# Four d_ff tiles beside the attention instead of five, the first input in two transfers, the low half of a pair in two pieces, and the sums added by 128 tokens

## The chip, the cores and the metric

The kernel runs on one core of a Trainium2 chip. Its time is the device time of one execution in microseconds (us). TensorE (PE in the profile) multiplies matrices, VectorE (DVE), ScalarE (ACT) and GpSimd (POOL) do elementwise work, and SyncE (SP) issues nearly all transfers.

## The reference

The input is a recurrence over 768 tokens for 4 sequences and 8 heads of 40 channels, and behind it a gated feed-forward layer on all 3072 tokens, with weights in 64-bit floats:

```python
for t in range(S):
    y[:, :, t] = np.einsum('bhd,bhde->bhe', rt, state)
    Sa = np.einsum('bhde,bhe->bhd', state, at)
    state_decay = state * wt[:, :, None, :] - np.einsum('bhd,bhe->bhde', Sa, bt)
    state = state_decay + np.einsum('bhd,bhe->bhde', vt, kt)
...
x = attn_out.transpose(0, 2, 1, 3).reshape(B * S, H * D)   # 3072 x 320
out = ((x @ w_a) * (x @ w_b)) @ w_out                      # d_ff = 1536
```

## The kernel before

**Blocks and batches.** The 768 tokens are cut into 12 blocks of 64. A block has 4 batches (one for each sequence), so the attention has 48 batches; the text counts them in the order in which they end. A batch goes through `prep` (two scans for the decay products, the scaled operands `A` and `BK`, the score matrix `pssc`, masked into `TT`), then the four batches of a block together through `lanes` (a triangular solve of 31 steps on VectorE, `Yt` and `psl`, with a way through device memory to turn the data, and the products `psw` and `pst`), then through `main` (`psr`, `psu`, `psg`, `psy`, and last the transposes `psyt`). `self_state` carries the state to the next block (`pss`, `psst`). When four batches of a block have ended, `xform` splits their output into a high and a low part in `xkr`, which holds two blocks.

**The feed-forward layer.** d_ff is cut into 12 tiles of 128. A unit is one tile for one block (256 tokens): 16 matmuls into `ab` (8 for w_a, 8 for w_b, by parts of the operands), a copy on ScalarE, the product on VectorE, a cast to the high part `gh` on ScalarE, the low part `gl` on GpSimd, and 6 matmuls into `po`. This text calls it a single. A `Pair` takes two blocks at once (512 tokens): 16 matmuls of 512 columns, and 12 into four banks. The first `F1` tiles are held in `ws1` from the start and run as singles while the attention runs, as far as a block's output is there; blocks 0 and 1 take only 2 and 3 of them then (`FIRST`) and the others later. Their sums go to device memory (`po_d`). After the attention the other tiles follow in groups of two (`groups`, in three sets of weights that are filled in turn), nearly all as pairs, and VectorE adds their sums onto the earlier ones (`fin2`, `acc`). Each tile of weights is decoded from 64-bit floats to two 32-bit parts by VectorE, ScalarE and GpSimd (`decode`, `w_ex`, `w_mt`, `w_rs`).

**What sets the order.** The class `Order` plans while the program is built: each part of the work is a generator that yields the engine and the tiles that its next step needs, and `run` takes the step that could start first by the plan's clock, plus a claim that puts it back (`after` with `WAY` and `NWAY` puts preparations of later blocks back; `LATER` the loading of weights). The engines then run their instructions in this order. Where the plan sees TensorE idle for over 0.8 us (`GAP`), `warm` puts matmuls of the identity with itself into the queue, into the tile that comes next (`pssc<-ident`, `ab<-ident`); their result is overwritten. This text calls them fillers. In the trace each filler is two records.

`F1`, `groups`, `all_units` and `moe` set which tile runs when; `prep` loads `I`; `Pair.whole` makes `gl` and ends a group; all of these carry lines of the change.

Of the kernel before, what the change touches and what calls it, by code (L numbers as in the profile page):

```python
# [10 lines left out]
F32 = mybir.dt.float32  # L11
# [9 lines left out]
B = 4  # L21
# [3 lines left out]
HB = 32  # L25
# [4 lines left out]
P = 128  # L30
NF = DFF // P
CW = NG * (C + 1)
PW = CW + 1 + NG * 3 * C
F1 = 5
FG = 2
# [3 lines left out]
NL = 12  # L39
WAY = 0.5  # L40
LATER = 1.5
NWAY = 1
URG = 0.05
NEAR = 0.05
FIRST = (2, 3)
AHEAD = 3
SPB = 2
# [5 lines left out]
VC = 0.2  # L53
WARM = 12
RAW = 2

# [4 lines left out]
SPARE = 1.0  # L61
HOP = 0.1
LAND = 2.4
# [11 lines left out]
class Order:  # L75
# [78 lines left out]

    def part(self, gen):
        self.parts.append([gen, None])
        self.step(self.parts[-1])
# [7 lines left out]
    def run(self):  # L165
        while self.parts:
            best = None
            for p in self.parts:
                e, deps, claim, may = p[1]
                if may is not None and not may():  # L170
                    continue
                at = max([self.now[e]] + [self.ready(x, e) for x in deps])
                t = at + (claim(at) if callable(claim) else claim)
# [130 lines left out]
def wkv_moe(ctx, tc, pin, rv, vn, wa, wb, wo, out):  # L304
    nc0 = tc.nc
    order = Order(tc, nc0)
    nc = order.nc
# [212 lines left out]
    class Pair(Unit):  # L520
# [16 lines left out]
        def whole(self):  # L537
# [142 lines left out]
    def prep(q):  # L680
# [79 lines left out]
    def lanes(n):  # L760
# [20 lines left out]
        done.blocks += 1  # L781
        yield "scalar", [nb0_d[n], nb1_d[n]], 0.0, lambda: done.at > SPB
        ps = at_take("psl")
        nc.scalar.copy(out=ps, in_=yid)
        Y = ps.rearrange("p (i t) -> p i t", t=HB)
        for s in range(HB - 1):
            ni, w = s // 2 + 1, HB - 1 - s
            Wv = W[:, 0:ni * w].rearrange("p (i t) -> p i t", i=ni)
            yield "vector", [N, Y], urgent, None
            nc.vector.tensor_mul(  # L790
                out=Wv, in0=Y[:, 0:ni, s:s + 1].to_broadcast([P, ni, w]),
                in1=N[:, s:s + 1, s + 1:].to_broadcast([P, ni, w]))
            yield "vector", [], urgent, None
            nc.vector.tensor_sub(out=Y[:, 0:ni, s + 1:], in0=Y[:, 0:ni, s + 1:], in1=Wv)
        yield "scalar", [Y], 0.0, None

        Y = N[:, 0:HB // 2]
        nc.scalar.copy(out=Y.rearrange("p i t -> p (i t)"), in_=ps)
        at_give(ps)
        eng = nc.scalar if n < TSQ else nc.sync  # L800
# [60 lines left out]
    def main(q):  # L861
# [49 lines left out]
        order.part(self_state(q, uvf, bkf, stf, st, sdf))  # L911
        yield "scalar", [ps, ps0], 0.0, None
# [51 lines left out]
    def self_state(q, uvf, bkf, stf, st, sdf):  # L964
        n, b = divmod(q, B)
        if n < NS - 1:
            yield "tensor", [uvf, bkf], 0.0, lambda: done.at > 0
            ps = at_take("pss")
# [62 lines left out]
    def fin2(n, last):  # L1031
        def f(po):
            for hf in range(2):
# [31 lines left out]
    def moe():  # L1065
# [3 lines left out]
        for n, kk, f, first, last, fin in all_units():  # L1069
            if isinstance(n, tuple):  # L1070
# [5 lines left out]
                u = Pair(lp[0], f"{n[0]}_{f}", x, dest(f), first, last, fin, 0.06)  # L1076
                order.part(u.whole())
                while not u.begun:
# [18 lines left out]
            u.by = "scalar" if kk < 0 else "vector"  # L1097
            order.part(u.whole())
            while not u.begun:
# [74 lines left out]
    for q in range(NS * B):  # L1174
        order.part(prep(q))
    for n in range(NS):
        order.part(lanes(n))
    for q in range(NS * B):
        order.part(values(q))
        order.part(others(q))  # L1180
        order.part(main(q))
    for n in range(NS):
        order.part(xform(n))
    order.part(all_weights())
    order.part(moe())
    order.part(early())
    order.part(late())
    order.part(judge())
# [101 lines left out]
```

## Time and profile before

| | |
|---|---|
| three runs | 956.69, 960.84 and 963.85 us, median 960.84 us |
| profiled execution | 963.8 us |
| its span, first to last instruction | 961.6 us, so 2.2 us lie around it |
| mean granted TensorE clock | 0.964 |
| PE, DVE, ACT, POOL busy | 927.0, 586.5, 436.8, 299.5 us |
| end of the last batch's transposes | 695.1 us into the span |

The busy time of PE counts the fillers. A matmul's record is longer than the time until the next one starts, since they overlap; so the time that a group of matmuls takes in the queue is read from the chain of waits, where a row gives the start and the length of a run of them. Nearly every row names line 190, the helper that records each operation, so rows are told apart by their tiles.

### The profile page before, as it was taken

What the parts mean: (1) busy time and instruction counts of PE and PEld (TensorE: products, weight loads), DVE (VectorE), ACT (ScalarE), POOL (GpSimd) and SP (SyncE); (2) the same over time, 40 slices, a digit from 0 to 9 for tenths busy, and PEclk for the clock granted to TensorE, in tenths of its full rate; (3) what the DMA queues carried; (4) which work ended last, traced back from release to release, by engine and by line L of the source; (5) the groups of instructions that cost most, each with busy time, mean ns of one, the idle gap of its engine ahead of it and who ended that gap; (6) DMA issues with size and microseconds to landing.
All of it is one profiled execution on the core that took longest, in us unless ns stands there. A gap on an engine that the chain in (4) does not pass through costs nothing.

```text
span 961.6 us, 23562 instructions
## 1 busy us (share of the span) xinstructions
PE 927.0 (96%) x9230; PEld 833.0 (87%) x9230; DVE 586.5 (61%) x1588; ACT 436.8 (45%) x1325; POOL 299.5 (31%) x405
## 2 busy tenths in 40 slices
PE   9999998999897999999999999999999999999996
PEld 9998977898786888888888889888999898888885
DVE  6877687668857767685869494723523646542333
ACT  4164456445663554655565655435533333322221
POOL 2130222123352332242323222213444445442221
PEclk9999989599995999999999999999999999999999
DMA  5454627464734553554655654347477411100013
GB/s 135 123 118 93 146 59 155 104 118 126 161 96 111 122 145 81 113 116 117 145 117 130 143 124 85 97 89 189 119 173 191 104 43 54 49 4 1 1 47 122
DMA packets 132946, 102.56 MB, mean 107 GB/s; under 512 B 86659, under 2 KB 118595, under 8 KB 132827
## 3 DMA queue, kind: packets, MB, share of 16 engines
q1 hardware_dynamic: 130747, 100.71, 44.6%
q8 instruction: 75, 1.23, 0.6%
q10 hardware_dynamic: 2080, 0.26, 0.2%
q14 instruction: 44, 0.36, 0.1%
HBM read 77.03 MB, written 21.94 MB: 103 GB/s over the span
## 4 chain that ended last, share of the span: by engine, by line
PE 73%; DVE 11%; DMA 5%; SPq 3%; issue 3%; POOL 3%; ACT 2%; DVEq 0%; POOLq 0%
PE ab L190 26%; PE po L190 9%; PE pssc L190 8%; PE psr L190 5%; PE psy L190 5%; PE psg L190 4%; PE ps L190 4%; SPq L190 3%; DVE psl L190 3%; DVE Yt L190 3%; PE pss L190 3%; PE psu L190 2%; DMA I<-in_pin_dram 2%; PE psw L190 2%; PE pst L190 2%
## 5 line engine op out<-in xcount | busy, mean ns | idle before, releaser
L190 POOL TENSOR_TENSOR gl<-asb,gh 128x256 fp32r<-128x256 f32 (+1 forms) x106 | 103.0, 972 | 253.7 <-ACT gh L190 241.6
L190 PE MATMUL ab<-xkr,wt 120*128 120x256 f32 (+1 forms) x1024 | 149.5, 298 | 0.0
L190 DVE TENSOR_TENSOR asb<-ab,asb 128x256 f32<-128x256 f32 (+1 forms) x104 | 53.3, 513 | 149.5 <-PE ab L190 88.9
L190 PE MATMUL ab<-xk,wt 120*128 120x512 f32 (+1 forms) x656 | 142.1, 368 | 0.0
L190 PEld LDWEIGHTS ab<-xkr,wt 120*128 120x128 f32 x1024 | 133.6, 192 | 4.9
L190 PEld LDWEIGHTS ab<-xk,wt 120*128 120x128 f32 x656 | 112.7, 188 | 19.1
L190 PE MATMUL po<-wo,gh 128*128 128x320 f32 x424 | 116.4, 322 | 4.5 <-ACT gh L190 4.4
L190 DVE TENSOR_TENSOR Yt<-psl,N 128x126 f32<-128x126 f32 (+22 forms) x372 | 94.1, 253 | 24.5 <-DMA N<-nb_d 13.1
L190 DVE TENSOR_TENSOR psl<-psl,Yt 128x126 f32<-128x126 f32 (+22 forms) x372 | 97.1, 261 | 11.6
L190 ACT CAST gh<-asb 128x256 fp32r<-128x256 f32 (+1 forms) x106 | 51.3, 484 | 110.2 <-DVE asb L190 109.0
L190 ACT COPY asb<-ab 128x256 f32<-128x256 f32 (+1 forms) x106 | 47.7, 450 | 106.3 <-PE ab L190 104.9
L190 PEld LDWEIGHTS po<-wo,gh 128*128 128x128 f32 x424 | 76.4, 190 | 7.8 <-ACT gh L190 5.2
L190 PE MATMUL po<-wo,gl 128*128 128x320 f32 x212 | 67.8, 320 | 5.5 <-POOL gl L190 5.3
L190 ACT ACTIVATE Abd<-A,m 120x192 f32<-120x192 f32 x144 | 54.9, 447 | 31.5 <-POOL A L190 29.4
L190 POOL TENSOR_TENSOR pe<-Pc,rp 120x192 f32<-120x192 f32 x44 | 25.2, 573 | 137.2 <-DVE rp L190 130.7
L190 PE MATMUL pssc<-ident 128*128 128x128 f32 x548 | 65.1, 280 | 1.4 <-POOL ident masks.py:199 1.4
L190 PEld LDWEIGHTS pssc<-ident 128*128 128x128 f32 x548 | 63.7, 196 | 1.6 <-POOL ident masks.py:199 1.4
L190 POOL TENSOR_TENSOR ST<-tmp,pcm 120x360 f32<-120x360 f32 x40 | 33.5, 837 | 94.3 <-DVE tmp L190 94.3
L190 PE MATMUL psg<-rvt 120*128 120x192 f32 (+1 forms) x288 | 53.0, 329 | 0.2 <-DVE tmp L190 0.2
L190 PE MATMUL pssc<-Abd,BK 120*128 120x192 f32 (+1 forms) x288 | 52.1, 319 | 1.1 <-ACT Abd L190 0.9
L190 DVE TENSOR_TENSOR TT<-pssc,tri 128x512 f32<-128x512 f32 x48 | 32.8, 686 | 29.3 <-PE pssc L190 29.2
L190 PEld LDWEIGHTS psg<-rvt 120*128 120x128 f32 x288 | 49.3, 205 | 0.9 <-DVE tmp L190 0.4
(131 smaller groups left out, 1774.0 us busy)
## 6 DMA issues: line engine op xcount, KB each, us to landing
rvt<-in_rv_dram SPq DMA_DIRECT2D x48, 450.0 KB
I<-in_pin_dram SPq DMA_DIRECT2D x46, 361.9 KB
xk_d<-xkr SPq DMA_DIRECT2D x11, 720.0 KB
xk<-xk_d SPq DMA_DIRECT2D x10, 720.0 KB
N<-nb_d SPq DMA_DIRECT2D x48, 128.0 KB
wraw<-in_wa_dram SPq DMA_DIRECT2D x12, 360.0 KB
wraw<-in_wb_dram SPq DMA_DIRECT2D x12, 360.0 KB
wraw<-in_wo_dram SPq DMA_DIRECT2D x12, 320.0 KB
```

Of the source, the lines that this page charges most:

```text
L190: r = fn(*args, **kwargs)
```

## The change

- `F1` is 4: four tiles are held and run as singles beside the attention; the other eight make four groups of two (before: seven, in three groups of two and one of one). Of the 144 tile-and-block products, 56 are singles and 88 lie in 44 pairs; before, 68 were singles and 76 lay in 38 pairs.
- The plan's numbers change: `WAY` 0.5 to 0.25, `NWAY` 1 to 2, `HOP` 0.1 to 0.13, `AHEAD` 3 to 4 (how many blocks ahead sums and inputs are loaded again after the attention).
- The first batch's input `I` (772 columns) comes in two transfers, the first 196 columns (which the scans read) and the other 576.
- In a pair, GpSimd makes `gl` in two halves of 256 columns.
- At the end of a pair's group, VectorE's step of adding two banks is planned as two steps of one bank (128 tokens) each, and a block's output transfer is put into SyncE's queue when its second bank is added.
- `HAND`, `CS` and `PLN` are new means to move a part by hand or to solve on GpSimd; with `{}`, `0.0` and `()` they move nothing.

```diff
-F1 = 5
+F1 = 4
...
-WAY = 0.5
+WAY = 0.25
 LATER = 1.5
-NWAY = 1
+NWAY = 2
...
-AHEAD = 3
+AHEAD = 4
...
+HAND = {}
+CS = 0.0
+PLN = ()
...
-HOP = 0.1
+HOP = 0.13
...
-            nc.gpsimd.tensor_sub(out=gl, in0=g, in1=gh.bitcast(F32))
+            for c in range(2):
+                sl = slice(c * 256, c * 256 + 256)
+                nc.gpsimd.tensor_sub(out=gl[:, sl], in0=g[:, sl], in1=gh[:, sl].bitcast(F32))
...
-                po, then = Unit.po, []
-                for i in range(2):
-                    yield "vector", po[2 * i:2 * i + 2], 0.0, None
-                    then.append(self.done[i](po[2 * i:2 * i + 2]))
+                po = Unit.po
+                for i in range(4):
+                    yield "vector", [po[i]], 0.0, None
+                    then = self.done[i // 2](po[i // 2 * 2:][:2], (i % 2,))
+                    if then and i % 2:
+                        nc.sync.dma_start(out=then[0], in_=then[1])
                 at_give(*po[2:])
                 Unit.po_free, Unit.po = True, None
-                for x in then:
-                    if x:
-                        nc.sync.dma_start(out=x[0], in_=x[1])
...
-        nc.sync.dma_start(out=I, in_=pin[n, b])
+        if q == 0:
+            nc.sync.dma_start(out=I[:, 0:CW + 1], in_=pin[n, b][:, 0:CW + 1])
+            nc.sync.dma_start(out=I[:, CW + 1:], in_=pin[n, b][:, CW + 1:])
+        else:
+            nc.sync.dma_start(out=I, in_=pin[n, b])
```

The change reorders TensorE's queue from the first block on. Behind the fourth batch (the end of block 0) TensorE's queue reads as follows before; `pssc` and `psn` with `Abd` and `BK` are the preparation of batches of a later block, `psyt` ends a batch, and the rows with `ident` alone are fillers:

```order
L190 MATMUL psyt<-ident,yn 120x64
L190 MATMUL pssc<-ident 128x128 x24
L190 MATMUL pssc<-Abd,BK 128x192 x2
L190 MATMUL pssc<-Abd,BK 128x128
L190 MATMUL psn<-ident,BK 128x120 x3
L190 MATMUL pssc<-ident 128x128 x23
L190 MATMUL pssc<-Abd,BK 128x192 x2
L190 MATMUL pssc<-Abd,BK 128x128
L190 MATMUL psn<-ident,BK 128x120 x3
L190 MATMUL pssc<-ident 128x128 x15
L190 MATMUL pssc<-Abd,BK 128x192 x2
L190 MATMUL pssc<-Abd,BK 128x128
```

And now, at the same place (`psw` and `pst` with `TT_173` belong to the solve of block 1):

```order
L193 MATMUL psyt<-ident,yn 120x64
L193 MATMUL psw<-ident 128x128 x3
L193 MATMUL psw<-W,TT_173 32x32 x16
L193 MATMUL psn<-ident,BK 128x120 x3
L193 MATMUL psw<-ident 128x128 x11
L193 MATMUL psw<-W,TT_173 32x32 x16
L193 MATMUL pssc<-ident 128x128 x11
L193 MATMUL pssc<-Abd,BK 128x192 x2
L193 MATMUL pssc<-Abd,BK 128x128
L193 MATMUL pst<-TT_173,W 32x32 x32
```

The products that finish block 1's solve stood behind several preparations of a later block and the fillers ahead of them (they do not come within these rows before); now only the second half of one preparation (`psn`) and one other preparation stand among them.

SyncE's queue begins before with whole inputs, `I` twice and then into the tiles `N` and `W`, and then the first weights and the first scores on their way to device memory:

```order
L190 DMA I<-in_pin_dram 120x772 x2
L190 DMA N<-in_pin_dram 120x772
L190 DMA W<-in_pin_dram 120x772
L190 DMA wraw<-in_wa_dram 120x768
L190 DMA wraw<-in_wb_dram 120x768
L190 DMA nb_d_115<-TT_172 32x5x32
```

And now:

```order
L193 DMA I<-in_pin_dram 120x196
L193 DMA I<-in_pin_dram 120x576
L193 DMA I<-in_pin_dram 120x772
L193 DMA N<-in_pin_dram 120x772
L193 DMA W<-in_pin_dram 120x772
L193 DMA wraw<-in_wa_dram 120x768
L193 DMA wraw<-in_wb_dram 120x768
```

One transfer more stands in front of the second batch's input; the rest keeps its place.

More of the change, by code (lines that the diff above doesn't have):

```diff
@@ L153, in tile, with part @@
         return x
-    def part(self, gen):
-        self.parts.append([gen, None])
+    def part(self, gen, key=""):
+        self.parts.append([gen, None, HAND.get(key, 0.0)])
         self.step(self.parts[-1])
@@ L781, in lanes @@
         done.blocks += 1
-        yield "scalar", [nb0_d[n], nb1_d[n]], 0.0, lambda: done.at > SPB
-        ps = at_take("psl")
+        solver = "gpsimd" if n in PLN else "vector"
+        eng = getattr(nc, solver)
+        if n in PLN:
+            yield "scalar", [nb0_d[n], nb1_d[n]], 0.0, None
+            ps = order.tile(pp, [P, HB // 2 * HB], F32, tag="Y", name="Y", bufs=1)
+        else:
+            yield "scalar", [nb0_d[n], nb1_d[n]], 0.0, lambda: done.at > SPB
+            ps = at_take("psl")
         nc.scalar.copy(out=ps, in_=yid)
@@ L788, in lanes @@
             Wv = W[:, 0:ni * w].rearrange("p (i t) -> p i t", i=ni)
[L789 to L790 removed]
+            yield solver, [N, Y], urgent, None
+            eng.tensor_mul(
                 out=Wv, in0=Y[:, 0:ni, s:s + 1].to_broadcast([P, ni, w]),
                 in1=N[:, s:s + 1, s + 1:].to_broadcast([P, ni, w]))
[L793 to L794 removed]
+            yield solver, [], urgent, None
+            eng.tensor_sub(out=Y[:, 0:ni, s + 1:], in0=Y[:, 0:ni, s + 1:], in1=Wv)
         yield "scalar", [Y], 0.0, None
         Y = N[:, 0:HB // 2]
[L798 to L799 removed]
+        if n in PLN:
+            Y = ps.rearrange("p (i t) -> p i t", t=HB)
+        else:
+            nc.scalar.copy(out=Y.rearrange("p i t -> p (i t)"), in_=ps)
+            at_give(ps)
         eng = nc.scalar if n < TSQ else nc.sync
@@ L910, in main @@
             transp(uT[g], uvf[p0:p0 + C, g * PK:(g + 1) * PK], C, p0)
-        order.part(self_state(q, uvf, bkf, stf, st, sdf))
+        order.part(self_state(q, uvf, bkf, stf, st, sdf), f"s{n}")
         yield "scalar", [ps, ps0], 0.0, None
@@ L966, in self_state @@
         if n < NS - 1:
-            yield "tensor", [uvf, bkf], 0.0, lambda: done.at > 0
+            yield "tensor", [uvf, bkf], CS * (n < 1), lambda: done.at > 0
             ps = at_take("pss")
@@ L1031, in fin2, with f @@
     def fin2(n, last):
-        def f(po):
-            for hf in range(2):
+        def f(po, hfs=range(2)):
+            for hf in hfs:
                 nc.vector.tensor_add(out=acc[n][:, hf, :], in0=po[hf][:, 0:DM], in1=acc[n][:, hf, :])
@@ L1076, in moe @@
                 u = Pair(lp[0], f"{n[0]}_{f}", x, dest(f), first, last, fin, 0.06)
-                order.part(u.whole())
+                order.part(u.whole(), f"u{n[0] if isinstance(n, tuple) else n}.{f}")
                 while not u.begun:
@@ L1097, in moe @@
             u.by = "scalar" if kk < 0 else "vector"
-            order.part(u.whole())
+            order.part(u.whole(), f"u{n[0] if isinstance(n, tuple) else n}.{f}")
             while not u.begun:
@@ L1174, in wkv_moe @@
     for q in range(NS * B):
-        order.part(prep(q))
+        order.part(prep(q), f"p{q // B}")
     for n in range(NS):
-        order.part(lanes(n))
+        order.part(lanes(n), f"l{n}")
     for q in range(NS * B):
-        order.part(values(q))
-        order.part(others(q))
-        order.part(main(q))
+        order.part(values(q), f"v{q // B}")
+        order.part(others(q), f"v{q // B}")
+        order.part(main(q), f"m{q}")
     for n in range(NS):
[L1183 to L1187, printed above, removed]
+        order.part(xform(n), f"x{n}")
+    order.part(all_weights(), "w")
+    order.part(moe(), "u")
+    order.part(early(), "e")
+    order.part(late(), "e")
     order.part(judge())
```

2 lines of the change are left out of this document (1 added, 1 removed).

## The prediction

> **What bounds the kernel now.** I read the page first, for who is busy when.
>
> ```profile
> span 961.6 us, 23562 instructions
> PE 927.0 (96%) x9230; PEld 833.0 (87%) x9230; DVE 586.5 (61%) x1588; ACT 436.8 (45%) x1325; POOL 299.5 (31%) x405
> PE   9999998999897999999999999999999999999996
> PEclk9999989599995999999999999999999999999999
> PE 73%; DVE 11%; DMA 5%; SPq 3%; issue 3%; POOL 3%; ACT 2%; DVEq 0%; POOLq 0%
> ```
>
> PE is busy nearly everywhere, and the chain of waits (last row) runs through it for 73%. But PE's queue holds fillers, so a busy PE is not yet a limit. I therefore cut the span at the end of every fourth batch (the last `psyt` of a block; the rows of blocks 4 and 11 are left out) and at the end of the attention, 695.1 us. The columns are the stretch, its length, busy time of PE, PEld, DVE, ACT and POOL with their instructions, the granted clock, the transfers' share and GB/s.
>
> ```profile
> 0.00:92.60 92.60, 89.33 (x954) 85.31 (x954) 68.38 (x200) 40.39 (x132) 18.89 (x52) 1.00 0.50 117
> 92.60:169.00 76.40, 70.25 (x793) 63.73 (x792) 57.23 (x163) 38.13 (x124) 22.88 (x37) 0.95 0.58 121
> 169.00:237.80 68.80, 67.57 (x723) 60.19 (x722) 49.45 (x149) 30.69 (x99) 17.54 (x24) 0.80 0.49 111
> 237.80:285.40 47.60, 43.12 (x524) 37.68 (x525) 35.41 (x83) 29.10 (x95) 21.64 (x30) 0.96 0.59 139
> ...
> 339.80:409.30 69.50, 67.41 (x781) 62.14 (x782) 44.92 (x136) 36.51 (x120) 20.14 (x30) 0.98 0.46 108
> 409.30:460.60 51.30, 49.80 (x640) 44.36 (x640) 36.62 (x111) 29.19 (x100) 16.10 (x24) 1.00 0.51 119
> 460.60:508.10 47.50, 46.72 (x602) 41.03 (x604) 34.27 (x100) 29.82 (x102) 13.46 (x22) 0.96 0.58 131
> 508.10:558.00 49.90, 49.10 (x553) 43.53 (x554) 35.05 (x106) 28.58 (x96) 15.31 (x24) 1.00 0.56 126
> 558.00:615.40 57.40, 56.95 (x733) 51.08 (x735) 40.55 (x128) 30.92 (x101) 14.56 (x21) 1.00 0.42 98
> 615.40:652.40 37.00, 37.00 (x510) 32.54 (x512) 12.02 (x32) 16.73 (x57) 7.26 (x9) 1.00 0.48 108
> ...
> 742.00:955.00 213.00, 212.06 (x1108) 186.14 (x1106) 98.10 (x196) 59.71 (x105) 78.89 (x68) 1.00 0.18 48
> ```
>
> Counted in the program, 453 of the 472 fillers stand ahead of the 24th batch (409.3 us), none from there to the 40th (615.4 us). So there are three stages. Up to 409 us PE waits for others, with fillers in the gaps; VectorE, 57.2 of 76.4 us in block 1, is the busiest of those. From 409 to 695 us PE is full of real work, 46.7 of 47.5 us in block 7 and 57.0 of 57.4 us in block 9, and VectorE is at 70 to 72% in blocks 6 to 9 (35.05/49.9, 34.27/47.5). After the attention PE is full too (212.06 of 213.00 us), the others are far from it.
>
> **Singles against pairs.** The chain of waits gives what a run of matmuls takes in PE's queue. Two rows for singles, four for pairs:
>
> ```profile
> 716.26 1.91 PE ab L190 x16
> 718.17 0.88 PE po L190 x6
> ...
> 897.50 3.65 PE ab L190 x16
> 901.15 0.88 PE po L190 x6
> 902.04 0.88 PE ps L190 x6
> 902.92 3.65 PE ab L190 x16
> ```
>
> A single is 1.91 + 0.88 = 2.79 us; a pair is 902.92 - 897.50 = 5.42 us, 2.71 for each block. Twelve singles become six pairs: 6 x 5.42 - 12 x 2.79 = 32.5 - 33.5 = **-1.0 us**. So the fifth tile is nearly only moved. Counted in the program, 41 singles begin ahead of the 48th batch's end in place of 50, which takes 9 x 2.79 = 25.1 us out of the attention; behind it stand 15 singles and 44 pairs in place of 18 and 38, which puts back 32.5 - 8.4 = 24.1 us. The removed singles are those of the PE-bound stage: 33 began there before, now 24, four in each block in place of 3 to 8.
>
> The Trainium skill ("TensorE: Matmul & The Clock Gate", Back-to-back issue gap) gives sustained spacings of about 81 ns at 128 columns and 131 ns at 512; by it, with an estimated 98 ns at 256, the change would save 12 x 16 x 98 - 6 x 16 x 131 ns = 6.2 us on `ab`. The rows here contradict it: 3.65 us for 16 is 228 ns at 512 columns, so this gets no chance of its own.
>
> **Fillers and order.** The program now has 460 fillers, not 472. Their price is that of the longest run of them, in the chain (188 records of 94 fillers and 6 others):
>
> ```profile
> 34.08 21.87 PE pssc L190 x194
> ```
>
> 21.87/194 = 0.113 us a record, two records a filler: 0.225 us. Twelve fewer are **-2.7 us**. They also move: 35 in place of 110 within block 1, 413 in place of 453 up to the 24th batch (-9.0 us), then 47 in place of 19 (+6.3 us). A filler says only that a gap was foreseen; I take the net, since a gap that is foreseen wrongly shows as a wait instead. What block 1 loses in fillers it loses because the end of its solve stands earlier. Before, the preparations that stood ahead of it waited for inputs, as the chain shows at that place:
>
> ```profile
> 111.98 3.70 DMA I<-in_pin_dram
> 119.45 4.11 DMA I<-in_pin_dram
> 123.57 2.40 DMA nb_d<-TT
> ```
>
> Those preparations come later now, so that their waits move behind block 1 rather than vanish; the fillers that blocks 2 and 3 gain (71 for 54, 27 for 1) say the same.
>
> **The fifth tile's decoding.** VectorE's five steps for twelve tiles (36 pieces):
>
> ```profile
> L190 DVE SCALAR_TENSOR_TENSOR w_rs<-wraw,w_ex 120x384 f32<-120x384 uint32 (+1 forms) x36 | 23.0, 639 | 0.0
> L190 DVE SCALAR_TENSOR_TENSOR w_ex<-wraw,w_ex 120x384 int32<-120x384 int32 (+1 forms) x36 | 22.0, 612 | 5.4 <-ACT w_ex L190 5.1
> L190 DVE TENSOR_TENSOR w_mt<-w_ex,w_mt 120x384 int32<-120x384 int32 (+1 forms) x36 | 20.1, 559 | 0.5
> L190 DVE TENSOR_SCALAR w_ex<-wraw 120x384 int32<-120x384 int32 (+1 forms) x36 | 20.1, 558 | 3.0 <-DMA wraw<-in_wa_dram 2.6
> L190 DVE TENSOR_SCALAR w_mt<-wraw 120x384 int32<-120x384 int32 (+1 forms) x36 | 16.6, 460 | 20.2 <-POOL wt L190 16.7 <-POOL wo L190 3.4
> ```
>
> 101.8/12 = 8.5 us a tile leave VectorE's early stage and go behind the attention, where VectorE is busy 98 of 213 us; there they cost nothing while the tile is ready a group ahead. In the early stage they are worth between 0 (done in gaps) and 8.5 us. I take 0 beyond the fillers, since the plan already counts a lighter VectorE in them. The tile's three loads move with it; they are in SyncE's queue, ahead of other inputs, within the same bounds.
>
> **The start.** VectorE's first scan waits for the whole first input:
>
> ```profile
> 0.82 0.87 SPq L190 DMA_DIRECT2D I<-in_pin_dram  x2
> 4.53 0.60 DVE L190 TENSOR_TENSOR_SCAN Pc<-I,one 120x195 f32<-120x195 f32 x1 [4.53 <-DMA I<-in_pin_dram]
> 7.17 0.56 DVE L190 TENSOR_TENSOR_SCAN Pc<-I,one 120x195 f32<-120x195 f32 x1
> ```
>
> The first transfer now has 196 of 772 columns. If the time to landing (4.53 - 0.82 = 3.71 us) went by size, the scan would start 2.8 us sooner; if size did not matter, not at all. The second batch's scan, at 7.17, needs an input that is issued one transfer (0.87/2 = 0.43 us) later, and that bounds what follows: -1.2 to +0.4 us, and I take **-0.6 us**. The other 576 columns, which the first batch's `A` reads, have the same bytes in front of them as before.
>
> **The end.** Behind the last pair's last products PE waits for `gl`:
>
> ```profile
> 951.83 1.27 POOL L190 TENSOR_TENSOR gl<-asb,gh 128x512 fp32r<-128x512 f32 x1 [4.20 <-ACT gh L190]
> 953.15 0.42 PE L190 MATMUL po<-wo,gl 128*128 128x320 f32 x1 [0.94 <-POOL gl L190]
> L190 POOL TENSOR_TENSOR gl<-asb,gh 128x256 fp32r<-128x256 f32 x68 | 53.2, 782 | 134.6 <-ACT gh L190 122.5 <-ACT rvt L190 9.0 <-DMA UV<-in_vn_dram 2.8
> ```
>
> A half takes 0.78 us in place of 1.27: **-0.5 us**; the second half ends 1.56 us after 951.83, at 953.39, when PE's third group (0.88 us after 952.66) needs it at 953.54. Elsewhere a pair costs GpSimd 1.56 - 1.27 = 0.29 us more, 44 pairs some 13 us, in a stage where it is busy 79 of 213 us and PE has the next unit's `ab` in between: 0. Adding by 128 tokens has the same additions in the same order at the end, and each output still waits for its second one: 0. `AHEAD` brings loads forward in a stage where PE waits 0.9 us in all: 0.
>
> **The sum**: -1.0 - 2.7 - 0.6 - 0.5 = -4.8 us. The profiled execution took 963.8 us, 3.0 us over the median of the three, so it would be 959.0; against the median, 960.84 - 4.8 = **956.0 us**.
>
> **Rivals.**
>
> *The early stage gains more* (faster). Up to 409 us VectorE and the inputs set the time. If all of the 8.5 us of decoding leave the path there, on top of the sum, it is 956.0 - 8.5 = 947.5 us. For it: VectorE at 75% in block 1 with PE on fillers. Against it: 40 fillers fewer there are already in the sum's -2.7.
>
> *The cover is lost* (slower). From 409 to 695 us singles fill PE while the attention's chain waits for ScalarE, VectorE and inputs. The nine singles that leave are 25.1 us. If PE then waits for the chain in part of this time, the attention does not shorten by it, while the 24.1 us behind it are paid in full. For it: block 3, with three singles and two records of fillers, had 43.1 of 47.6 us busy, and DVE at 74%. Against it: blocks 7 and 10, with three singles each, had PE busy for 46.7 of 47.5 and 37.0 of 37.0 us. It turns the sign when 4.8 of the 25.1 us stay as waits; with two thirds, 16.7, the time is 972.7 us.
>
> *The clock falls.* These rows of 40 us have a low clock; the chain's rows show the same kind of matmuls inside and outside of such a stretch:
>
> ```profile
> 160.00:200.00 40.00, 36.77 (x390) 32.17 (x391) 27.60 (x89) 16.26 (x53) 8.16 (x13) 0.66 0.51 107
> 280.00:320.00 40.00, 34.84 (x388) 29.37 (x383) 26.81 (x90) 18.95 (x60) 9.57 (x14) 0.74 0.43 101
> 147.17 1.48 PE psr L190 x22
> 177.66 7.39 PE psr L190 x53
> ```
>
> 67 ns a matmul become 139 ns. With 75 fillers fewer in block 1 another stretch of some 27 us at half clock ((1 - 0.66)/0.5 x 40) can come. PE's work in it would last 13.6 us longer, half of which, 6.8 us, I count, since PE waits for others early: 962.8 us. The Trainium skill ("TensorE: Matmul & The Clock Gate", HAM oscillation) says that an idle gap over about 3.4 us throws the clock back to half; it speaks against taking fillers out. The trace agrees in part: in both low rows PE is idle, for 3.2 and 5.2 of 40 us, though no row shows the length of a single gap.
>
> **How the numbers follow.** Chances: forecast 0.45 (its own range 949 to 963: the start's and the fillers' bounds, and waits that come out a few us otherwise), early gain 0.26 (943 to 952), cover lost 0.15 (966 to 982), clock 0.14 (959 to 970). The three runs lie 0.75% apart, so about 1% (9.6 us: under 951.2 or over 970.4) can be told from no change. Faster by over 1%: nearly all of the early gain and a quarter of the forecast's own range, 0.24 + 0.11 = 0.35. Slower by over 1%: most of the lost cover and a little of the clock, 0.13. Within: 0.52. The range 941 to 970 leaves out the upper part of the lost cover (0.13) and the far end of an early gain (0.05).
>
> **What would show it.** Cutting the new trace at the same batches: the 24th batch should end some 4 to 10 us before 409, the attention near 695.1 - 25.1 - 2.7 = 667 us, and from there PE should be full for 955.0 - 695.1 + 24.1 = 284 us. Lost cover shows as PE's busy share falling under 95% in blocks 6 to 10; the clock as a row under 0.9 that wasn't there; an early gain as a 24th batch before 398 us. If PE waits for `wt` of a late group, the tile's decoding was not free. The prediction is wrong if the attention ends later than 680 us or the stage behind it is not some 24 us longer.

## The result and the profile after

| | kernel before | changed kernel |
|---|---|---|
| median of 20 runs each, taken together | 961.53 us (956.69 to 968.14) | 966.56 us (961.51 to 974.4) |
| ratio, 95% interval | | 1.0067 (1.0046 to 1.0089) |
| profiled execution, its span | 963.8, 961.6 us | 970.14, 968.1 us |
| end of the 24th, 40th, 44th, 48th batch | 409.3, 615.4, 652.4, 695.1 us | 384.3, 573.3, 641.1, 679.0 us |

The change made the kernel slower by 0.7%, where 0.5% faster was forecast. The time is inside the range, but the sign is wrong. The chip has a second, slower state that a few executions fall into; ratios and intervals, here and below, leave these out and medians do not, so that a ratio need not be the quotient of two medians. The page of the changed kernel:

```profile
span 968.1 us, 23364 instructions
PE 928.1 (96%) x9110; PEld 831.2 (86%) x9110; DVE 594.2 (61%) x1582; ACT 435.2 (45%) x1313; POOL 305.6 (32%) x443
PE   9997999998999999999998999799999999999997
PEclk9997899998989999999999799679999999999999
```

It reads almost like the page of before, but for a hole in the 26th of the 40 slices: PE at 7 tenths, and a granted clock of 6 tenths there and 7 in the next. The cut at the ends of every fourth batch (columns as in the prediction; the rows of blocks 2 to 7 are left out) puts it in its place:

```profile
0.00:107.50 107.50, 100.00 (x980) 95.09 (x980) 83.17 (x235) 43.49 (x138) 26.34 (x60) 0.92 0.53 116
107.50:156.00 48.50, 47.44 (x602) 42.06 (x602) 37.70 (x109) 29.38 (x100) 15.69 (x23) 1.00 0.60 141
...
473.50:530.80 57.30, 52.54 (x673) 45.72 (x674) 43.10 (x133) 32.72 (x110) 14.95 (x25) 0.99 0.58 132
530.80:573.30 42.50, 41.10 (x462) 36.40 (x464) 24.11 (x72) 21.41 (x73) 9.73 (x14) 0.82 0.49 102
573.30:641.10 67.80, 58.49 (x671) 50.58 (x670) 26.55 (x76) 25.45 (x80) 13.43 (x16) 0.78 0.45 104
641.10:679.00 37.90, 37.66 (x395) 33.73 (x396) 14.75 (x31) 16.90 (x54) 12.97 (x14) 0.99 0.44 121
679.00:961.80 282.80, 282.42 (x1564) 251.67 (x1564) 125.49 (x247) 84.05 (x159) 114.50 (x141) 1.00 0.27 67
```

At the 40th batch the changed kernel is 42.1 us ahead of the kernel before (573.3 against 615.4). Block 10 then takes 67.8 us, with PE idle for 9.3 of them and the clock at 0.78; before it took 37.0 us, though for 510 matmuls in place of 671. The stage behind the attention is 22.9 us longer (282.8 against 259.9), as the tile that was moved there asks.

SyncE's queue shows what happened in block 10. First the changed kernel, then the kernel before at the same place in the program (start, length of the issue, what is loaded):

```profile
598.37 2.49 SPq L193 DMA_DIRECT2D UV<-in_vn_dram  x4
618.46 0.80 SPq L193 DMA_DIRECT2D xk<-xk_d  x2
619.30 0.41 SPq L193 DMA_DIRECT2D wraw<-in_wa_dram  x1
```

```profile
649.69 1.21 SPq L190 DMA_DIRECT2D UV<-in_vn_dram  x2
651.98 0.80 SPq L190 DMA_DIRECT2D xk<-xk_d  x2
652.82 0.41 SPq L190 DMA_DIRECT2D wraw<-in_wa_dram  x1
```

`xk<-xk_d` loads a block's inputs of the feed-forward layer again, for the stage behind the attention (`early`). It goes into memory that the preparations held, and so waits for their last user, a `pst` of PE. In the changed kernel it stands in the queue from 600.86 us and is let go at 618.4:

```profile
SPq L193 <- PE pst L193: 17.5, 1, 17.5
```

Behind it stands the raw form of the first late tile's weights, `wraw<-in_wa_dram`. SyncE issues its queue in order, and the weights go out at 619.30 us, right behind `xk`, though no wait of their own is seen there. What that does to the other engines (start, length, in brackets the idle time ahead and what ended it):

```profile
629.04 0.36 DVE L193 TENSOR_SCALAR w_ex<-wraw 120x384 int32<-120x384 int32 x1 [11.16 <-DMA wraw<-in_wa_dram]
629.43 0.61 ACT L193 ACTIVATE w_ex<-w_ex,bias 120x384 int32<-120x384 int32 x1 [10.24 <-DVE w_ex L193]
630.34 0.62 ACT L193 COPY yn<-psy 64x240 f32<-64x240 f32 x2
631.01 0.76 PE L193 MATMUL psyt<-ident,yn 128*120 128x128 f32 x2 [8.74 <-ACT yn L193]
```

The chain of waits names the transfer as the longest piece of that time:

```profile
619.30 9.71 DMA wraw<-in_wa_dram
```

VectorE holds the decoding at the head of its queue and waits 11.16 us for it; ScalarE waits 10.24 us for VectorE with its part of the decoding; behind that in ScalarE's queue stands the copy `yn`, which has nothing to do with the weights; and PE, whose next instruction is the transpose of `yn`, stands for 8.74 us. In the kernel before `xk` went out 1.1 us behind the load ahead of it and the weights right after, and the wait for them was 2.6 us (its row is in the prediction). There the first late tile's decoding stood behind the 44th batch, now it stands behind the 42nd; so the stretch to compare is block 11 of the kernel before, in which PE never stood:

```profile
652.40:695.10 42.70, 42.70 (x455) 38.17 (x455) 20.14 (x42) 21.60 (x66) 17.05 (x18) 1.00 0.61 148
```

**A ledger of PE's queue.** To tell waits from work, each matmul's time until the next one starts was counted as work up to what its kind takes undisturbed (115 ns for a filler's record, 235 and 125 ns for `ab` of 512 and 256 columns, 150 ns for `po`, 210 ns for the attention's), and what is over that as remainder: waits, and part of a slow clock. In us, from the profiled execution of each kernel, "weights first" being the first experiment below:

| | before | after | weights first |
|---|---|---|---|
| singles and pairs (`ab`, `po`) | 397.1 | 396.5 | 396.8 |
| fillers | 105.5 | 102.8 | 102.7 |
| the attention's matmuls | 383.3 | 384.3 | 378.0 |
| remainder up to the 24th batch | 48.3 | 37.6 | 41.9 |
| remainder, 24th to 48th batch | 17.2 | 37.5 | 23.7 |
| remainder behind the attention | 2.0 | 1.1 | 1.1 |
| end of PE's last matmul | 955.0 | 961.8 | 945.7 |

The two terms that the prediction worked out from counts stand in it, with signs and sizes: 2.7 us for the fillers (-2.7 forecast) and 0.6 us for pairs in place of singles (-1.0). The remainder decides.

### The profile page after: what moved, and what is told of

It reads as the page before. It is cut to its first block, busy times and chain, and to the rows that moved or that the text cites. A ratio compares the mean times of both kernels' runs of the same rounds, so it can differ in the third digit from the quotient of the medians.

```text
span 968.1 us, 23364 instructions
## 1 busy us (share of the span) xinstructions
PE 928.1 (96%) x9110; PEld 831.2 (86%) x9110; DVE 594.2 (61%) x1582; ACT 435.2 (45%) x1313; POOL 305.6 (32%) x443
## 4 chain that ended last, share of the span: by engine, by line
PE 77%; DVE 11%; DMA 4%; issue 2%; ACT 2%; SPq 1%; POOL 1%; POOLq 0%; DVEq 0%; ACTq 0%
PE ab L193 26%; PE pssc L193 9%; PE po L193 9%; PE psr L193 6%; PE ps L193 4%; PE psg L193 4%; PE psy L193 4%; DVE psl L193 4%; DVE Yt L193 4%; PE pss L193 3%; PE psu L193 3%; PE psw L193 2%; PE psyt L193 2%; SPq L193 1%; PE pst L193 1%
## 5 line engine op out<-in xcount | busy, mean ns | idle before, releaser
L193 POOL TENSOR_TENSOR gl<-asb,gh 128x256 fp32r<-128x256 f32 x144 | 108.5, 766 | 270.3 <-ACT gh L193 270.1
L193 PE MATMUL ab<-xk,wt 120*128 120x512 f32 (+1 forms) x696 | 155.5, 375 | 0.0
L193 PEld LDWEIGHTS ab<-xk,wt 120*128 120x128 f32 x696 | 121.9, 188 | 21.9
L193 PE MATMUL ab<-xkr,wt 120*128 120x256 f32 (+1 forms) x872 | 136.8, 305 | 3.5 <-DMA xkr<-lo 3.5
L193 PEld LDWEIGHTS ab<-xkr,wt 120*128 120x128 f32 x872 | 118.2, 195 | 9.0 <-DMA xkr<-lo 4.2
L193 PE MATMUL po<-wo,gh 128*128 128x320 f32 x400 | 110.5, 322 | 0.0
L193 DVE TENSOR_TENSOR psl<-psl,Yt 128x126 f32<-128x126 f32 (+22 forms) x372 | 97.2, 261 | 11.8
L193 PEld LDWEIGHTS po<-wo,gh 128*128 128x128 f32 x400 | 72.2, 190 | 3.0
L193 PE MATMUL po<-wo,gl 128*128 128x320 f32 x200 | 63.2, 316 | 1.2 <-POOL gl L193 1.2
L193 PE MATMUL psg<-rvt 120*128 120x192 f32 (+1 forms) x288 | 57.8, 345 | 0.2 <-ACT rvt L193 0.2
L193 ACT COPY yn<-psy 64x240 f32<-64x240 f32 (+1 forms) x96 | 29.0, 302 | 57.5 <-PE psy L193 56.8
```

Source lines behind the costliest of these rows:

```text
L193: r = fn(*args, **kwargs)
```

## The experiments

Two theories stood against each other. The **wait theory**: the changed kernel loses its time in block 10, to the weights that stand behind `xk` in SyncE's queue; without that it is faster than before. The **cover theory**, from the prediction's rivals: PE lacks the nine singles that left the attention (the first expectation below says ten; it is nine), and what is seen in block 10 is only where that shows.

**The weights ahead of the reloads.** In the changed kernel the reloads of `xk` may enter the queue only when the first late tile's weights have been issued. PE's queue is the same up to the 45th batch, and so are VectorE's and ScalarE's.

```diff
         for n in range(NE):
-            yield "sync", [xk_d[n]], 0.1, None
+            yield "sync", [xk_d[n]], 0.1, lambda: F1 in ready_w
             load_x(ep, n)
```

> The changed kernel with one thing moved: the two reloads of earlier blocks (xk, 720 KB each), which stand in SyncE's queue ahead of the first weights of the late groups, are put behind them. TensorE's queue is the same up to the 45th batch. Wait theory (VectorE's first decoding step stands at the head of its queue and waits 11.2 us for weights that SyncE could not issue, and the attention's steps wait behind it): the wait of w_ex for wraw falls from 11.2 to under 3 us and the time from 966.6 to 954 to 959 us. Cover theory (the ten singles that left filled TensorE, and the attention's own chain is now the limit): nothing changes, 964 to 969 us, and the attention ends at 679 us as before the move.

Measured: 954.46 us, 0.9944 (0.9915 to 0.9974) of the kernel before. SyncE's queue in block 10, the decoding, and the cut from the 40th batch on:

```profile
601.80 2.49 SPq L193 DMA_DIRECT2D UV<-in_vn_dram  x4
604.33 0.59 SPq L193 DMA_DIRECT2D wraw<-in_wa_dram  x1
```

```profile
615.82 0.35 DVE L193 TENSOR_SCALAR w_ex<-wraw 120x384 int32<-120x384 int32 x1
```

```profile
576.70:625.50 48.80, 48.23 (x671) 41.94 (x671) 26.70 (x75) 25.21 (x79) 12.64 (x15) 1.00 0.43 102
625.50:662.80 37.30, 37.06 (x396) 33.36 (x395) 13.48 (x31) 16.96 (x55) 13.66 (x16) 1.00 0.56 148
662.80:945.70 282.90, 282.52 (x1565) 251.72 (x1564) 124.73 (x247) 83.87 (x159) 114.55 (x142) 1.00 0.27 71
```

The weights go out 0.04 us behind the load ahead of them, VectorE finds them there when it comes to them, and block 10 takes 48.8 us in place of 67.8, with the same 671 matmuls. The wait theory holds: one order in SyncE's queue is worth 1.0067 - 0.9944 = 1.2%, or 11.8 us, and turns the sign. What was planned anew behind the 45th batch is not the reason, for the stretches there are as long as in the changed kernel (37.3 and 282.9 us against 37.9 and 282.8).

**The weights later.** The other way out of block 10: the first late tile is loaded and decoded only near the attention's end.

```diff
-                    len(sets) > 2 if kk == 0 else ...
+                    len(sets) > 2 and done.y >= NS * B - 2 if kk == 0 else ...
```

> The changed kernel with the late groups' weights held back until 46 batches have ended, so that none of their decoding stands in the queues of VectorE and ScalarE while the attention runs, but the reloads of xk keep their place. Wait theory: as in the run with weights first, 954 to 960 us; TensorE may then wait a few us for the first late tile. Cover theory: 964 to 969 us.

Measured: 971.67 us, 1.0124 (1.0084 to 1.0165). Block 10 takes 48.8 us here too, and the attention ends at 661.6 us; so far the wait theory is right. But the stage behind it is 300.4 us long, not 283 (the ledger's remainder there is 18.6 us, not 1.1). Waits of that stage:

```profile
DVE w_ex L193 <- DMA wraw<-in_wb_dram: 9.6, 1, 9.6
...
PE ab L193 <- DMA wt<-wt: 7.3, 1, 7.3
```

The wait was only moved. Decoding the tile at the end of the attention, amid the reloads, costs more than in block 10. The expected 954 to 960 us were wrong: I had looked only at the wait that went.

**Four tiles alone.** The kernel before with one number changed, and the same with weights first:

```diff
-F1 = 5
+F1 = 4
```

> The kernel before with four tiles held instead of five, and nothing else. Its plan equals that of the kernel before up to the fifth tile's weights, and its first late decoding step stands behind the 44th batch, as in the kernel before. Cover theory: four tiles cost time by themselves, 966 us or more against 961.5. Wait theory: four tiles cost nothing, the sum of the prediction holds here (1.0 us less for pairs, 20 fillers less at 0.225 us), 953 to 961 us.

> The kernel before with four tiles in the attention and weights first. The kernel before with four tiles alone took 1.0216 of the kernel before, with a wait of PE for reloaded wt of 7.8 us behind the attention. If the place of the reloads in SyncE's queue decides there too, the time depends on whether they end ahead of the attention's end: with them out of the way, 0.995 to 1.003; with the reloads pushed against the attention's end (as in the kernel before with weights first, where wt took 9.6 us to land), 1.012 to 1.025 as before. I think the second likelier.

Measured: 981.71 us, 1.0216 (1.0178 to 1.0255); with weights first 973.62 us, 1.0165 (1.0116 to 1.0214). The 953 to 961 us of the wait theory for the first did not come out, the cover theory's "966 us or more" did; for the second it was the worse of the two outcomes, which had been thought the likelier. The chain of waits of the first behind the attention:

```profile
693.21 10.05 DMA wt<-wt
```

(With weights first this piece is 8.14 us.) PE waits for decoded weights that go through device memory and land amid the reloads. That explains 8 to 12 us of remainder behind the attention. The cover theory has its part as well: from the 24th to the 48th batch the remainder is 31.1 and 33.6 us, against 17.2 in the kernel before. So of the 25.1 us of singles that left, 14 to 16 come back as remainder. That is not all waiting: PE's idle time there is 10.8 and 12.5 us against 3.5, and 7 and 10 us of the added remainder lie in stretches at half clock, of which these two executions have 23.9 and 30.7 us there and the kernel before 3.4.

**Five tiles with all the rest of the change**, without and with weights first:

```diff
-F1 = 4
+F1 = 5
```

> The changed kernel with five tiles held again: the plan's other numbers, the split input and the halves stay. The reloads of xk stand ahead of weights with four batches' inputs still to come, as in the changed kernel. Wait theory: it has the same kind of wait near the attention's end and is not faster than the changed kernel by more than 3 us, 962 to 970 us. Cover theory: with the fifth tile back beside the attention it is faster by 5 us or more, 955 to 961 us.

> The changed kernel with five tiles in the attention instead of four, and with the reloads of xk behind the first late tile's weights in SyncE's queue (the edit of the run with weights first). So it has neither the wait nor the move of a tile. By the prediction's term for singles against pairs, four tiles are worth 1.0 us over five once the wait is gone: 0.9956 of the kernel before, some 956 to 957 us, with the attention's end 25 us later than with four tiles (near 688 us) and 259 us behind it. Theory of lost cover (PE needs the nine singles in the attention): five tiles are then the better, 948 to 952 us. Theory that the four tiles themselves do harm elsewhere: also under 952. If the order is scattered by 1% whatever is changed, it is over 962.

Measured: 976.62 us, 1.0145 (1.0094 to 1.0197), slower than either theory had it; and with weights first 965.26 us, 1.0051 (1.0021 to 1.0081), over 962 us, as expected there if orders scatter by 1%. Waits of the first in blocks 10 and 11:

```profile
DVE w_ex L193 <- DMA wraw<-in_wa_dram: 11.8, 1, 11.8
...
PE psyt L193 <- ACT yn L193: 9.1, 1, 9.1
```

The wait is there with five tiles too, and taking it away is worth 0.9%, or 9.0 us; again it is block 10 that shortens (61.5 to 49.2 us), and what lies behind it hardly changes (38.9 and 259.1 us against 37.1 and 260.3). So it is not the moved tile that brings the wait, but the rest of the change: most likely the planner's new numbers, which put the reload and the decoding earlier against the attention. No run changed these numbers alone. Without the wait four tiles beat five by 1.0051 - 0.9944 = 1.1%, against the 0.1% expected: the five-tile order has 14 singles in its first 24 batches where the four-tile order has 17, at nearly the same time (386.6 and 387.4 us), and a remainder of 31.3 in place of 23.7 us behind them. Four tiles are better with the new numbers, and worse with the old ones.

**Weights first in the kernel before.**

> The kernel before with only the edit that lets xk's reloads go behind the first late tile's weights. Its wait for these weights was 2.6 us, and PE had no idle time from it (37.00 of 37.00 us busy in block 10). Wait theory: nothing to win there, 958 to 963 us, ratio 0.997 to 1.003; so the gain of weights first in the changed kernel comes from the wait which the four tiles made. Rival: weights first is a gain by itself, and what made the changed kernel with it faster is not the change: 951 to 955 us here.

Measured: 967.13 us, 1.008 (1.0046 to 1.0114). Weights first is thus no gain by itself, which the wait theory needs; but it is a loss of 0.8%, where 0.997 to 1.003 was expected. The chain of waits behind the attention:

```profile
700.76 9.57 DMA wt<-wt
```

In the kernel before, this `wt` is issued at 699.3 and 700.2 us and the next reloads from 705.7 on; here the second half of `wt` is issued at 700.76 us, and two reloads, pushed back, 5.6 and 1.5 us ahead of it.

**The first input, and the fillers ahead of it.** The changed kernel with weights first, once with the first input in one transfer (all other queues unchanged), once with no fillers ahead of the first mask, by which all that follows is planned anew:

```diff
-        if q == 0:
-            nc.sync.dma_start(out=I[:, 0:CW + 1], in_=pin[n, b][:, 0:CW + 1])
-            nc.sync.dma_start(out=I[:, CW + 1:], in_=pin[n, b][:, CW + 1:])
-        else:
-            nc.sync.dma_start(out=I, in_=pin[n, b])
+        nc.sync.dma_start(out=I, in_=pin[n, b])
```

```diff
-        if order.turn != "tensor" or done.x >= WARM:
+        if order.turn != "tensor" or done.x >= WARM or done.mask == 0:
```

> The changed kernel with weights first, and the first input in one transfer again; all other orders of PE, VectorE, ScalarE and GpSimd stay row by row. Prediction's term: the split was worth 0.6 us (0 to 1.2), so 955.1 us against 954.5 with the split. Theory from the trace after: the fillers ahead of the first mask eat the gain, so nothing at all, 954 to 955 with the first product of real data at the same time as with the split (near 11.9 us at a slow clock). Against both: the split is worth 2 us or more, 956.5 and over.

> The changed kernel with weights first and no fillers ahead of the first mask; the order behind is planned anew from there, with 369 fillers in place of 460. If the fillers ahead of the first mask hold up the start, the first product of real data comes at 8.5 to 9.5 us instead of 11.9, and the time is 1.5 to 3 us less, 951 to 953. Rival (the fillers keep the clock up): the clock stays at half for longer in the first 100 us, and the gain at the start is lost again: 955 to 965. By the price of a filler in the prediction, 91 fewer would be 20 us less, 934; I give that little weight, since most fillers stand where PE waits anyway.

Measured: 952.93 us, 0.9936 (0.991 to 0.9963) with one transfer, the same as with two (0.9944); 963.76 us, 1.0032 (0.9999 to 1.0065) without the first fillers. The start of the changed kernel, of the one with one transfer, and of the one without the first fillers:

```profile
1.45 10.60 PE L193 MATMUL pssc<-ident 128*128 128x128 f32 x68 [1.45 <-POOL ident masks.py:199]
2.94 0.56 DVE L193 TENSOR_TENSOR_SCAN Pc<-I,one 120x195 f32<-120x195 f32 x1 [2.94 <-POOL m L193]
11.88 1.04 PE L193 MATMUL pssc<-Abd,BK 120*128 120x192 f32 x6
```

```profile
4.69 0.56 DVE L193 TENSOR_TENSOR_SCAN Pc<-I,one 120x195 f32<-120x195 f32 x1 [4.69 <-DMA I<-in_pin_dram]
...
11.44 1.04 PE L193 MATMUL pssc<-Abd,BK 120*128 120x192 f32 x6
```

```profile
9.03 2.05 PE L193 MATMUL pssc<-Abd,BK 120*128 120x192 f32 x6 [9.03 <-DVE BK L193]
```

The split does start the first scan 1.75 us sooner, but PE's first real product stands behind 34 fillers, which end at about the same time either way. Without them it comes at 9.03 us, 2.85 us sooner, but the first six products then take 2.05 us in place of 1.04, which fits the rival in the expectation (the fillers keep the clock up). Besides, there is a remainder of 15.9 us behind the attention in place of 1.1, in a rest that was planned anew; so what those fillers cost in the end can't be told from this run.

**`gl` in halves alone.** The kernel before with the two halves. All queues are the same up to the attention's end; behind it, besides GpSimd's, some steps of VectorE, ScalarE and TensorE change places, which the expectation had not foreseen.

```diff
-            nc.gpsimd.tensor_sub(out=gl, in0=g, in1=gh.bitcast(F32))
+            for c in range(2):
+                sl = slice(c * 256, c * 256 + 256)
+                nc.gpsimd.tensor_sub(out=gl[:, sl], in0=g[:, sl], in1=gh[:, sl].bitcast(F32))
```

> The kernel before with only gl of a pair in two halves; no other engine's order changes. The prediction's term: 0.5 us less, 0.9995 of the kernel before, with 8.95 to 9.3 us from the last gl to the span's end in place of 9.77, and nothing from GpSimd's 0.29 us more a pair. Rival: the longer gl delays po within the late stage, where PE then waits in the 38 pairs: 3 to 10 us more.

Measured: 958.79 us, 0.9998 (0.9963 to 1.0033), which can't resolve half a microsecond. The trace can; here the last `gl` of this kernel and of the changed one:

```profile
944.36 1.42 POOL L190 TENSOR_TENSOR gl<-asb,gh 128x256 fp32r<-128x256 f32 x2 [4.07 <-ACT gh L190]
```

```profile
959.15 1.42 POOL L193 TENSOR_TENSOR gl<-asb,gh 128x256 fp32r<-128x256 f32 x2 [4.07 <-ACT gh L193]
```

From there to the span's end it is 953.6 - 944.36 = 9.24 and 968.1 - 959.15 = 8.95 us, against 961.6 - 951.83 = 9.77 before: -0.5 and -0.8 us. The stage behind the attention is 259.4 us here, 259.9 before, so no cost of the longer `gl` elsewhere shows.

**A new order with nothing of the change.** How far does the time move when only the planner's number `HOP` moves by 0.01? Once in the kernel before (0.10 to 0.11), once in the changed kernel with weights first (0.13 to 0.12).

> The kernel before with one number of the planner (HOP, what a step from one engine to another costs) at 0.11 in place of 0.10, and 573 fillers. Nothing of the change is in it; it measures how much a new order is worth by itself. If orders scatter little, it is within 0.5% of the kernel before, 955 to 965 us; if scatter is as large as what weights first did in the kernel before, it is off by 0.5 to 1.5% on either side. By the price of a filler in the prediction, 101 more would be 22.7 us, 983; I expect at most a quarter of that, since fillers stand where PE waits.

> The changed kernel with weights first and HOP at 0.12 in place of 0.13, with 421 fillers in place of 460. Wait theory: no wait for the first late tile's weights, so 0.990 to 0.999 of the kernel before like the other two orders of the changed kernel without that wait. If a new order scatters by 1% either way, it is between 0.985 and 1.006, and the gain of 0.6% cannot be put down to the change's parts.

Measured: 982.26 us, 1.0233 (1.0195 to 1.027), and 961.23 us, 1.0004 (0.9976 to 1.0033). In the first the ledger has 22.6 us more of fillers (the 22.7 us of the prediction's price, of which I had expected at most a quarter) and 12.4 us more of remainder behind the attention, again with a transfer of `wt` that takes 9 us to land (9.29 us in the chain of waits); the attention's matmuls take 9.4 us less. The second kernel has no wait in block 10, but a remainder of 31.6 us from the 24th to the 48th batch and 8.1 behind the attention, and its gain is gone. Against the expectation, VectorE does wait there for the first late tiles' weights, in block 11, for 7.1 and 4.6 us, with no reload just ahead of them: weights first does not rule such a wait out.

So the time hangs on how the planner's order happens to fall, by up to 2.3% for one number moved by a hundredth. That bounds what may be concluded: that the wait in block 10, with what it does to the clock, costs 9 to 12 us is shown, since it was taken away with four tiles and with five, PE's order being held up to the 45th and the 46th batch; that four tiles, or any other single edit, are worth 0.6% is not. Part of the 9 to 12 us is clock: the mean granted clock of the executions is 0.962 with the wait and 0.968 without it (0.950 and 0.955 with five tiles), and among the executions of one of these kernels 0.01 of clock goes with 5 to 8 us of span. By that, an estimated 7 us of either difference is left at the same clock.

## Why the prediction was wrong

**The step that failed** is the cost of the moved loads and decoding: "The tile's three loads move with it; they are in SyncE's queue, ahead of other inputs, within the same bounds", 0 to 8.5 us gained, taken as 0. Two things were missed. First, the sign: a load can be held by what stands ahead of it. I asked what the tile's loads are ahead of, not what they are behind, and the reload of `xk` ahead of them waits for memory. Second, the reach: from SyncE the wait went through VectorE and ScalarE to PE in four steps, each engine holding an unrelated piece of the attention behind its part of the decoding. I had also said that a late decoding shows as PE waiting for `wt` of a late group; it showed as a wait for `yn` in block 10. It cost 9 to 12 us by the ratios, where the sum as a whole was missed by 10 us (-4.8 forecast, +5.0 measured). In the profiled execution block 10 took 19.0 us more than with weights first: 9.3 of 67.8 us idle there against 0.6 of 48.8, and the rest, 10.3 us, goes with the slow clock. As the wait is there with five tiles too, the step was too narrow as well: it asked about one moved tile, and the sum has no term for where the new order puts the reloads and the loads of all late tiles.

Without the wait the kernel comes to 0.9944, or -5.4 us, close to the forecast's -4.8. That is luck. Against the kernel before, the ledger's terms with weights first (one execution of each, 9.3 us apart) are -0.3 us for singles and pairs and -2.8 for fillers, near the forecast, but also -5.3 for the attention's matmuls, -6.4 for the remainder up to the 24th batch, +6.5 from there to the 48th and -0.9 behind the attention; of these four the sum had nothing but the start's -0.6.

**The move out of the attention** (9 x 2.79 = 25.1 us): singles and pairs between the 24th and the 48th batch fell from 91.6 to 68.2 us, -23.4. With 6.1 us more of fillers (6.3 forecast) that would have been -17.3; the stretch became 8.9 us longer instead. Of the 26.2 us between, 13.8 us are remainder that goes with weights first (37.5 against 23.7), 5.3 us slow matmuls of the attention that go with it too, 6.5 us remainder that stays (23.7 against 17.2), and 0.6 us others. The 6.5 us are where the rival *cover lost* would show, a quarter of the 25.1 us at most: PE's idle time in this stretch is 8.4 us with weights first against 3.5, but 3.5 of the 6.5 us lie in a stretch at half clock, and whether the lost cover set that off is open. Where the tiles were changed with the old numbers it was 14 to 16 us, in part slow clock too. The rival's mark, PE under 95%, was met in block 8 (52.54 of 57.30 us) besides block 10.

**The early stage.** Forecast: the 24th batch 4 to 10 us sooner; it came 25.0 us sooner in the profiled executions, which is the rival *early gain* with its mark (ahead of 398 us). Executions with the same order up to there scatter: 409.3, 407.0 and 403.9 us for the order of the kernel before (three kernels have it), 384.3 to 387.4 us for that of the changed one (four), so that the gain is some 17 to 25 us. The ledger gives 8.8 us to fillers (-9.0 forecast), 10.7 us to less remainder and 4.7 us to the attention's matmuls, which ran in a slower clock before (0.80 in block 2). With old numbers and four tiles the 24th batch came at 399.3 and 389.5 us (one order, executed twice), with new numbers and five tiles and three singles fewer at 388.3 and 386.6 us; so both edits seem to do it, and their shares stay open. That early gain and lost cover can come together is what I did not see: a lighter early stage moves the attention forward, and then, I think, it has less to fill PE with; no run shows this link by itself.

**The start** was forecast at -0.6 us (bounds -1.2 to +0.4). PE's first real product came at 11.88 us, where it had come at 10.49 before, and no gain of the split shows: the bounds were taken on VectorE, and the fillers ahead on PE were not looked at. **The tail** (-0.5) and **the stage behind the attention** (+24.1 forecast, +22.9) were right.

**The clock** as a rival was priced at +6.8 us for one more stretch. It came: the mean granted clock is 0.962 over the changed kernel's executions and 0.970 over those of the kernel before, which at 6 to 7 us for 0.01 makes an estimated 5 us, as much as the whole loss. But 0.006 of the 0.008 are not there with weights first, so most of it comes along with the wait. In the profiled execution PE stands from 622.3 to 631.0 us, the clock is half from 625.0 us on, and it stays half for the first 11 us of work behind the wait. The rule of the Trainium skill ("TensorE: Matmul & The Clock Gate", HAM oscillation) foresees a half clock for an idle gap of over 3.4 us; the trace agrees for this gap of 8.74 us.

## What to carry to other kernels

When work is moved, write down for each of its loads what stands ahead of it in the issuing queue and what that waits for; a load held by another's wait for memory stopped engines here that needed neither. Where an order is planned, compare a change with a few neighbouring orders before its gain or loss is put down to what was changed: here a hundredth in one number of the planner moved the time by 2.3%. A lighter stage pays only if the next one can use the time; keep filling work for the place where the chain gets thin.

## What the runs showed of the chip

A slow clock was seen without an idle PE ahead of it, as far as the records tell (a matmul's end is modelled in them). In the changed kernel, ahead of the wait and inside it (columns as above):

```profile
595.00:604.00 9.00, 9.00 (x145) 7.48 (x141) 2.57 (x6) 4.24 (x12) 0.72 (x1) 1.00 0.54 123
604.00:618.00 14.00, 14.00 (x157) 12.40 (x153) 1.76 (x3) 4.12 (x16) 0.84 (x2) 0.52 0.01 2
618.00:631.00 13.00, 4.27 (x53) 3.85 (x48) 1.55 (x5) 2.24 (x6) 0.74 (x1) 0.76 0.85 196
631.00:642.00 11.00, 10.99 (x79) 9.05 (x79) 6.14 (x13) 5.51 (x14) 4.68 (x5) 0.50 0.50 126
```

With weights first, the same place in PE's queue (3.4 us later, as its 40th batch ended at 576.7 us, not 573.3):

```profile
607.40:621.40 14.00, 14.00 (x227) 12.30 (x221) 6.04 (x12) 8.23 (x26) 3.35 (x4) 1.00 0.20 48
```

From 604 to 618 us PE was busy throughout, and had been for 9.00 of 9.00 us, yet 157 matmuls ran at a clock of 0.52 where the other run has 227 at 1.00. What set it off is open. It is likely why the profiled execution shows 19.0 us in block 10 where the ratios give 9 to 12.

A transfer of weights that went out with the reloads took 8 to 10 us to land (9.71, 9.57, 10.05, 9.29 and 8.14 us in five kernels); the DMA engines were at 0.85 of their time in the stretch from 618 to 631 us above. In each of them reloads had been issued up to 5.2 us ahead, which I take for the reason. The first late tile's weights bear it out: with reloads up to 2 us ahead of them in the queue they took 8.8 to 10.9 us in five kernels, and with none within 6 us 3.6 to 6.0 us in five others. But reloads are not the only way to a slow landing: a later load of weights in the changed kernel with weights first and `HOP` 0.12 took 8.61 us with no reload, but two other inputs, just ahead.
